# A gated attention and low-rank mixer kernel: the first slot with identity matmuls, smaller first loads and pairs on one engine

## The chip, the cores and the metric

The kernel runs on one core of one Trainium2 chip. The metric is the device time of one execution in microseconds, from its start to its last output; before the change it is 992.4 (median of three runs, 991.75 to 994.2). The engines are TensorE (PE in the profile, with PEld for its weight loads), VectorE (DVE), ScalarE (ACT), GpSimd (POOL) and SyncE (SP), which issues the DMAs. TensorE writes only PSUM; the others work on the on-chip memory, and VectorE and ScalarE read PSUM too.

## The reference, cut to what matters

Batch B = 8, sequence S = 3136, width D = 256, d_qk = 64, rank 32.

```python
def _attn_ref(u, v, z):
    scale = 1.0 / S
    scores = scale * np.matmul(z, z.transpose(0, 2, 1))
    attn = np.maximum(scores, 0.0) ** 2
    out = np.matmul(attn, v)
    return (u * out).astype(np.float32)

def _moe_ref(x, U, V, w_ch1, w_ch2):
    xt = x.transpose(0, 2, 1)
    h = xt @ U @ V
    u = x + h.transpose(0, 2, 1)
    ch = np.maximum(u @ w_ch1, 0.0) @ w_ch2
    return (u + ch).astype(np.float32)
```

The output is `_moe_ref` of `x = _attn_ref(u, v, z)`. The scores of one batch are a symmetric matrix of 3136 x 3136, which is made rectified and squared in bf16 and multiplied with v.

## The kernel before

**Tiles and items.** The sequence is 24 whole tiles of 128 rows and a tail of 64. Four tiles make a group: six groups of 512 columns and one of 64 for each batch. An item is a batch and a group, and the main loop (line 1203) runs through the 56 items; one pass is called a slot. In the slot of item (b, g) TensorE makes AV for that item, that is the squared scores of 512 output rows times v, and, between these matmuls, scores for the items to come and the mixer of items that lie behind. The mixer begins with batch 1, so that the first seven slots have only AV and scores.

**Row halves and ways.** z is kept transposed twice, once in each half of the 128 partitions (`zzT`), so that two matmuls of 64 rows run side by side, on the upper and the lower rows of the array. `pair` (line 173) issues such two. AV also goes in two halves of its 128 inner rows, each crossing two PSUM banks. One assignment of halves to banks is a way. `Ways` (line 567) runs along the 24 tiles in one way, 48 places, and at a turn changes to the other. When the halves change banks, a small GpSimd instruction (`post`, line 164, which shows as `POOLq L168`) stands behind the last matmuls and the next ones wait for it. It stands in GpSimd's own queue, behind any cast issued there before.

**Score pairs.** A score job makes 128 x 1024 scores: two key tiles (the two halves) against the 512 columns of a group. `rectify` (line 350) then writes relu(scale * s) from PSUM as bf16, on ScalarE (line 358) or, when VectorE has the shorter queue by the planner's books, on VectorE (line 354). `square` (line 346) multiplies the result with itself in place, always on VectorE, and is held back until the relu is due. For batch 0, groups 0 to 3, all 12 blocks of a group are made directly (`made_twice`); elsewhere, half of the blocks come from a DMA transpose. For batch 0 the job "last" makes the scores against the tail of the keys.

**The planner.** The program is issued in an order that a planner works out while the kernel is built. `clock` counts TensorE's time in units of one 256-column matmul pair, and `free_at` holds until when each of ScalarE, VectorE and SP is booked. `take_ps` takes the PSUM buffer, of four, that comes free first by these books. `emit` (line 971) goes through the AV places of a slot and issues from three queues what has its place there: `qc` (mixer), `qs` (scores) and `qm` (others). Each entry is a place, how many PSUM buffers must be free, whether the ways turn there, and a function. At a turn (line 979) `emit` also issues some of the `spare` casts on GpSimd: four, or two once the clock is over 200.

**The first slot.** What stands ahead of the main loop (lines 1102 to 1177) loads batch 0: z in three pieces of eight tiles (`first_z`) and v in six pieces of four tiles (`first_v`), all on SP's queue, casts them to bf16 and turns z. A z piece is cast twice (`cast_z`, c = 0 and 1), once for each half of the partitions. z is turned on TensorE: `z_turn` (line 311) multiplies each of eight tiles by the identity `ident` into PSUM and copies 128 x 1024 to `zzT` on ScalarE. Piece 0 is cast by VectorE and ScalarE; v0, z1, v1, v2 and z2 are cast by GpSimd in this order; v3, the tail and v4, v5 are spare casts. Then the first four score pairs come with their engines and times written out by hand (line 1157), then the second `z_turn`, and the planner's clock is set to 90. In slot 0 the other scores stand at places 8, 8, 26, 38, 42, 56, 64, 72, 80 (line 1282) and two each at 16, 46 and nA - 2, where the ways turn; the third and fourth `z_turn` stand at places 22 and 34.

Of the kernel before, what the change touches and what calls it, by code (L numbers as in the profile page):

```python
# [18 lines left out]
def kernel(  # L19
# [11 lines left out]
    nc = tc.nc  # L31
# [85 lines left out]
    def hold(due, f):  # L117
        held.append((due, len(held), f))
# [109 lines left out]
    def z_copy(b, t0, n, raw, c, copy):  # L228
        copy(out=z_bfs[b][:, t0 : t0 + n, c, :], in_=raw[:, : n * dqk].rearrange("p (t d) -> p t d", d=dqk))  # L229
# [18 lines left out]
    def v_copy(b, k, raw, copy):  # L248
        copy(out=v_bfs[b][:, k * GT : (k + 1) * GT, :], in_=raw.rearrange("p (t d) -> p t d", d=D))  # L249
        v_cast.add((b, k))  # L250
# [57 lines left out]
        )  # L308
        queued(NT * P / 4, True)

    def z_turn(b, t0, copy):
        n = min(2 * GT, NT - t0)
        k, pz = take_ps()
        for q in range(n):
            nc.tensor.matmul(  # L315
                out=pz[:, q // GT, (q % GT) * P : (q % GT + 1) * P],
                lhsT=z_bfs[b][:, t0 + q, :, :].rearrange("p c d -> p (c d)"),
                rhs=ident,
                start=(q % GT == 0),
                stop=(q % GT == GT - 1 or q == n - 1),  # L320
            )
        flat = pz.rearrange("p a c -> p (a c)")
        dst = zzTs[b].rearrange("p t c -> p (t c)")[:, t0 * P : (t0 + n) * P]
        copy(out=dst, in_=flat[:, : n * P])  # L324
        pe(8)
        ps_free[k] = book("act", clock[0] + 3, 9.5)
# [19 lines left out]
    def square(a, cost=6.3):  # L346
        book("dve", clock[0], cost)
        nc.vector.tensor_tensor(out=a, in0=a, in1=a, op=ALU.mult)  # L348

    def rectify(dst, src, part=1):  # L350

        ready = clock[0] + 3
        if max(free_at["dve"], ready) + 8 * part < max(free_at["act"], ready):
            nc.vector.tensor_scalar(  # L354
                out=dst, in0=src, scalar1=scale, scalar2=0.0, op0=ALU.mult, op1=ALU.max
            )
            return book("dve", ready, 11.2 if part == 1 else 6.4)
        nc.scalar.activation(out=dst, in_=src, func=AF.Relu, scale=scale)  # L358
        return book("act", ready, 8.7 if part == 1 else 5.3)

    def made_twice(b, g, J):
        return b == 0 and (g <= FIRST or J == g - 1)
# [78 lines left out]
    def score_finish(made):  # L446
        for dst, k, ps, turn, key in made:
            if key and split(*key):
                score_finish_split(dst, k, ps, turn, key)
                continue  # L450
            if turn:
                J, g, b = turn
                unturned[blocks[b, g, J][0]] = False
            done = rectify(dst, ps)
            ps_free[k] = done

            def finish(dst=dst, turn=turn, key=key):
                square(dst)
                if key:
                    squared[key] = squared.get(key, 0) + 1  # L460
                if turn:
                    hold(clock[0] + 7, lambda: ready_turns.append(turn))

            hold(done, finish)

    def score_finish_split(flat, k, ps, h, key):
        if h:
            done = rectify(
                flat[:, 2 * GW : 3 * GW].rearrange("p (j c) -> p j c", c=hw), ps[:, :, :hw], 0.5
            )  # L470
            a, cost = flat[:, 2 * GW : 3 * GW], 3.7
        else:
            done = rectify(
                flat[:, : 2 * GW].rearrange("p (w j c) -> p j w c", w=2, j=2),
                ps.rearrange("p j (w c) -> p j w c", w=2),
            )
# [626 lines left out]
    zraw = [(i * 2 * GT, 2 * GT + (i == 2), *stage_block()) for i in range(3)]  # L1103
    vraw = [stage_block() for _ in range(NQ)]

    def first_v(i):
# [5 lines left out]
    def cast_z(i, c, copy):  # L1112
        t0, n, entry, raw = zraw[i]
        z_copy(0, t0, 2 * GT, raw, c, copy)

    def cast_v(i, copy):
        v_copy(0, i, vraw[i][1], copy)
        give_block(vraw[i][0])

    def cast_tail(copy):  # L1120
        t0, n, entry, raw = zraw[2]
        for c in range(2):
            copy(out=z_bfs[0][:, NF, c, :], in_=raw[:, 2 * GT * dqk : n * dqk])
        v_tail(0, n, raw, copy)
        give_block(entry)

    first_z(0)
# [12 lines left out]
    on_act, on_dve, on_pool = nc.scalar.copy, nc.vector.tensor_copy, nc.gpsimd.tensor_copy  # L1140
    cast_v(0, on_pool)
    cast_z(1, 0, on_pool)
    cast_z(1, 1, on_pool)
    cast_v(1, on_pool)
    cast_v(2, on_pool)
    cast_z(2, 0, on_pool)
    cast_z(2, 1, on_pool)
    spare += [lambda: cast_v(3, on_pool), lambda: cast_tail(on_pool)]
    spare += [lambda i=i: cast_v(i, on_pool) for i in range(4, NQ)]

    cast_z(0, 0, on_dve)
    cast_z(0, 1, on_act)
    clock[0] = 40
    z_turn(0, 0, on_act)
    clock[0] = 58
    made = score_pairs(jobs_of(0, 0)[0:4])
    for (dst, k, ps, _, key), eng, done in zip(made, ("act", "dve", "act", "act"), (73, 79, 82, 92)):
        if eng == "act":
            nc.scalar.activation(out=dst, in_=ps, func=AF.Relu, scale=scale)
        else:  # L1160
            nc.vector.tensor_scalar(out=dst, in0=ps, scalar1=scale, scalar2=0.0, op0=ALU.mult, op1=ALU.max)
        ps_free[k] = done

    def square_first(i):
        dst, _, _, _, key = made[i]
        square(dst)
        squared[key] = squared.get(key, 0) + 1

    square_first(0)
    square_first(1)  # L1170
    z_turn(0, 2 * GT, on_act)
    square_first(2)
    square_first(3)
    for i in range(2):
        give_block(zraw[i][2])
    clock[0] = 90
    free_at.update(act=102, dve=104)

    todo = {t: [] for t in range(n_items)}
    for b in range(B):  # L1180
# [22 lines left out]
    for t in range(n_items):  # L1203
# [68 lines left out]
        elif av:  # L1272
# [105 lines left out]
```

## Time and profile before

| what | value |
|---|---|
| median of three runs | 992.4 us |
| lowest and highest | 991.75 and 994.2 us |
| the profiled execution | 994.29 us |
| its span in the profile | 992.5 us |
| TensorE clock granted | 1.00 in every stage |
| AV of slot 0 multiplied by u (line 694, first row) | starts at 31.40 us |
| the same of slots 1, 2, 3, 4 | 46.09, 59.84, 72.13, 87.02 us |

The span is the time from the first to the last thing that the profile shows; 1.8 us of the execution lie around it. A row of the timeline names the engine, the line of the kernel, the operation, output and input by the program's names, shapes and how many instructions were merged. In brackets stands how long the engine had been idle before the row and what ended that. A busy TensorE is not one at full speed: the rows of TensorE cover a matmul from its start to its modelled end. The granted clock in the profile's stage table is 1.00 from the first microsecond on, so a slow stretch is seen only in the durations of like rows.

### The profile page before, as it was taken

The numbers are of one execution on the slowest core, as the hardware profiler recorded it, in microseconds if no ns is written. First come the engines' busy times: TensorE is split into PE (matmuls) and PEld (weight loads), VectorE is DVE, ScalarE is ACT, GpSimd is POOL, SyncE is SP. The second block draws the span as 40 slices with busy tenths as digits, with TensorE's granted clock in tenths as the row PEclk, the third lists the DMA queues.
The fourth block names the chain that finished last, engine by engine and source line by source line (L and its number), as shares of the span: only waits on it lengthen the run. The fifth ranks groups of instructions, "written<-read, shape, count | busy, mean of one in ns | idle before, by whom it ended". The sixth has DMA issues, their size and how long they took to land.

```text
span 992.5 us, 35366 instructions
## 1 busy us (share of the span) xinstructions
PE 973.9 (98%) x16137; PEld 781.0 (79%) x16137; DVE 618.2 (62%) x793; ACT 491.4 (50%) x584; POOL 17.3 (2%) x24
## 2 busy tenths in 40 slices
PE   6999999999999999999999999999999999999997
PEld 3898788877778777787778877788777877787776
DVE  5977765668556675566756667555765666643453
ACT  5887742457324573355533465434653256422353
POOL 4100000000000000000000000000000000000000
PEclk9999999999999999999999999999999999999999
DMA  7999999889997799787998799975999889964142
GB/s 246 192 213 226 199 205 213 196 145 216 211 181 165 168 215 203 198 139 180 215 213 173 131 192 211 209 169 130 206 230 189 150 170 168 166 123 103 46 110 91
DMA packets 371974, 176.38 MB, mean 178 GB/s; under 512 B 347248, under 2 KB 350320, under 8 KB 371824
## 3 DMA queue, kind: packets, MB, share of 16 engines
q1 hardware_dynamic: 371824, 174.12, 86.8%
q8 instruction: 126, 2.06, 0.9%
q14 instruction: 24, 0.20, 0.1%
HBM read 62.56 MB, written 25.69 MB: 89 GB/s over the span
## 4 chain that ended last, share of the span: by engine, by line
PE 96%; DMA 1%; DVE 1%; ACT 1%; issue 0%; POOL 0%; SPq 0%; POOLq 0%; ACTq 0%
PE ps L178 93%; PE ps L661 1%; PE ps L742 1%; DMA blk<-in_v_dram 1%; DVE blk L348 1%; DMA u2T<-x_bf 0%; ACT blk L358 0%; PE ps L957 0%; ACT blk L906 0%; POOL z_bf L229 0%; DVE blk L354 0%; DVE blk L943 0%; DVE x_bf L694 0%; POOL v_bf L249 0%; PE ps L315 0%
## 5 line engine op out<-in xcount | busy, mean ns | idle before, releaser
L178 PEld LDWEIGHTS <-blk 64*128 64x128 bf16 x12288 | 617.2, 94 | 149.0 <-POOLq L168 7.7
L178 PE MATMUL ps<-v_bf,blk 64*128 64x256 bf16 x9216 | 612.6, 269 | 3.6 <-DVE blk L348 1.8
L358 ACT ACTIVATE blk<-ps 128x1024 bf16<-128x1024 f32 x339 | 319.6, 974 | 365.6 <-PE ps L178 354.2
L348 DVE TENSOR_TENSOR blk<-blk 128x1024 bf16<-128x1024 bf16 x352 | 226.4, 666 | 42.7 <-ACT blk L358 42.1
L178 PE MATMUL ps<-u2T,w_bf 64*128 64x512 bf16 (+1 forms) x1792 | 236.9, 349 | 0.5 <-DMA u2T<-x_bf 0.3
L178 PE MATMUL ps<-w_bf,blk 64*128 64x256 bf16 x3072 | 193.7, 269 | 0.2
L903 DVE TENSOR_SCALAR blk<-ps 128x1024 bf16<-128x1024 f32 (+1 forms) x110 | 127.1, 1155 | 92.9 <-PE ps L178 92.9
L906 ACT ACTIVATE blk<-ps 128x1024 bf16<-128x1024 f32 (+1 forms) x114 | 97.7, 866 | 91.6 <-PE ps L178 91.2
L178 PE MATMUL ps<-zzT 64*128 64x512 bf16 (+2 forms) x902 | 130.2, 329 | 1.7 <-ACT zzT L324 1.7
L178 PEld LDWEIGHTS <-w_bf 64*128 64x128 bf16 x1792 | 90.5, 94 | 29.2 <-POOLq L168 4.1
L694 DVE TENSOR_TENSOR x_bf<-ps,u_sb 128x1024 bf16<-128x1024 f32 x48 | 58.7, 1224 | 70.7 <-PE ps L178 70.7
L815 DVE TENSOR_TENSOR out_sb<-ps,x_bf 128x1024 f32<-128x1024 f32 (+1 forms) x49 | 54.2, 1107 | 59.3 <-PE ps L178 59.3
L943 DVE TENSOR_TENSOR out_sb<-ps,out_sb 128x1024 f32<-128x1024 f32 x42 | 51.3, 1222 | 18.3 <-PE ps L178 18.3
L178 PEld LDWEIGHTS <-zzT 64*128 64x128 bf16 x902 | 41.8, 95 | 8.0 <-ACT zzT L324 2.2
L178 PE MATMUL ps<-t_sb,V_bf 64*128 64x256 bf16 x200 | 20.8, 269 | 0.0
L198 ACT CAST x_bf<-out_sb 128x1024 bf16<-128x1024 f32 (+1 forms) x21 | 17.3, 826 | 6.0 <-DVE out_sb L815 6.0
L200 DVE CAST v_bf<-stage 128x1024 bf16<-128x1024 f32 (+1 forms) x33 | 20.2, 611 | 0.0
L178 PE MATMUL ps<-v_bf,last_sb 64*128 64x256 bf16 x192 | 18.6, 269 | 0.0
L354 DVE TENSOR_SCALAR blk<-ps 128x1024 bf16<-128x1024 f32 (+1 forms) x9 | 10.0, 1106 | 12.9 <-PE ps L178 12.9
L943 DVE TENSOR_TENSOR blk<-ps,blk 128x1024 f32<-128x1024 f32 x6 | 7.3, 1225 | 16.0 <-PE ps L178 15.9
L682 DVE TENSOR_TENSOR u_sb<-ps,u_sb 64x512 f32<-64x512 f32 x8 | 5.5, 682 | 17.1 <-ACT u_sb L680 17.1
L198 ACT CAST v_bf<-stage 128x1024 bf16<-128x1024 f32 x15 | 15.6, 1040 | 0.0
(67 smaller groups left out, 227.7 us busy)
## 6 DMA issues: line engine op xcount, KB each, us to landing
u_sb<-in_u_dram SPq DMA_DIRECT2D x48, 512.0 KB, 5.3
stage<-in_v_dram SPq DMA_DIRECT2D x42, 512.0 KB, 6.2
out_dram<-out_sb SPq DMA_DIRECT2D x42, 512.0 KB, 3.1
stage<-in_z_dram SPq DMA_DIRECT2D x7, 512.0 KB, 6.0
blk<-in_v_dram SPq DMA_DIRECT2D x6, 512.0 KB, 7.1
out_dram<-blk SPq DMA_DIRECT2D x6, 512.0 KB, 2.6
blk<-blk SPq DMA_TRANSPOSE x156, 5.2
blk<-in_moe_w_ch_dram SPq DMA_DIRECT2D x4, 512.0 KB, 5.5
```

The costliest lines, as they stand in the source:

```text
L178: ins = nc.tensor.matmul(**args)
L198: nc.scalar.copy(out=out, in_=in_)
L200: nc.vector.tensor_copy(out=out, in_=in_)
L348: nc.vector.tensor_tensor(out=a, in0=a, in1=a, op=ALU.mult)
L354: nc.vector.tensor_scalar(out=dst, in0=src, scalar1=scale, scalar2=0.0, op0=ALU.mult, op1=ALU.max)
L358: nc.scalar.activation(out=dst, in_=src, func=AF.Relu, scale=scale)
L661: nc.tensor.matmul(out=ps[c * hp : c * hp + rows, h, :D], lhsT=smalls[b][h * hp : (h + 1) * hp, place_of(jt), :], rhs=v_bfs[b][h * hp : (h ...
L694: nc.vector.tensor_tensor(out=xs[b, g][:rows, :n, :], in0=four(box["ps"])[:rows, :n, :], in1=u_sbs[b, g][:rows, :n, :], op=ALU.mult,)
L815: nc.vector.tensor_tensor(out=o[:rows, :n, :], in0=four(ps)[:rows, :n, :], in1=x, op=ALU.add)
L903: nc.vector.tensor_single_scalar(out=r, in_=ps[:, :, :gw], scalar=0.0, op=ALU.max)
L906: nc.scalar.activation(out=r, in_=ps[:, :, :gw], func=AF.Relu)
L943: nc.vector.tensor_tensor(out=o, in0=acc, in1=o, op=ALU.add)
```

## The change

- The z load of the first piece is split into two of four tiles each, the load of the first v piece into two of two tiles each (`load_run`). The two v0 loads go ahead of the second z piece. v4 and v5 go ahead of the first u load.
- Eighteen matmuls of the identity with itself, 128 columns each, are issued on TensorE as soon as the identity is there.
- The first half of z piece 0 is cast by VectorE (c = 0) and ScalarE (c = 1), the second half by VectorE twice. Two `z_turn` of four tiles each take the place of one of eight.
- `rectify` can put a pair whole on one engine, for full pairs of batch 0 that aren't split: VectorE relu and square in one go (`one_pass`), or ScalarE Relu and Square, or as before relu on ScalarE and square on VectorE. It takes the way that ends first by the books.
- The first four pairs go through this choice, and no longer by a list written out by hand. The planner's clock starts at 61 and no longer at 90.
- The second `z_turn` goes from ahead of AV to place 8 of slot 0, with a turn of ways; the third to 32 and the fourth to 58. z piece 2 is cast at place 26 by ScalarE and VectorE, and the tail at place 50 by VectorE, and no longer by GpSimd.
- In slot 0 the ways turn at places 8, 24, 40, 56, 72 and 88, with one score pair at each from 24 on; ten more pairs stand between. One spare cast is issued at each turn in slot 0, and two in later slots.
- `cast_v` for batch 0 casts a piece in two halves.

```diff
-    def z_turn(b, t0, copy):
-        n = min(2 * GT, NT - t0)
+    def z_turn(b, t0, copy, n=2 * GT):
+        n = min(n, NT - t0)
...
-    def rectify(dst, src, part=1):
+    def rectify(dst, src, b, part=1, whole=False):
 
         ready = clock[0] + 3
-        if max(free_at["dve"], ready) + 8 * part < max(free_at["act"], ready):
+        dve, act = max(free_at["dve"], ready), max(free_at["act"], ready)
+        if whole and not b:
+            slow = 10 if slot[0] == 0 else 6.3
+            ends = {"dve": dve + DVE, "act": act + 17.4, "both": max(act + 8.7, dve) + slow}
+            way = min(ends, key=lambda w: ends[w])
+            if way == "dve":
+                return one_pass(dst, src, ready)
+            if way == "act":
+                nc.scalar.activation(out=dst, in_=src, func=AF.Relu, scale=scale)
+                nc.scalar.activation(out=dst, in_=dst, func=AF.Square)
+                done = book("act", ready, 8.7)
+                book("act", ready, 8.7)
+                return done, free_at["act"]
+        elif dve + 8 * part < act:
...
+    DVE = 20
+
+    def one_pass(dst, src, ready):
+
+        nc.vector.tensor_scalar(out=dst, in0=src, scalar1=scale, scalar2=0.0, op0=ALU.mult, op1=ALU.max)
+        done = book("dve", ready, 11.2)
+        square(dst, 9)
+        return done, free_at["dve"]
...
-                for f in spare[: 2 if clock[0] > 200 else 4]:
+                for f in spare[: 2 if slot[0] else 1]:
...
+    for h in range(2):
+        load_run(zraw[0][3], z[0], dqk, h * GT, GT)
     make_identity(nc, ident)
+    for h in range(2):
+        load_run(vraw[0][1], v[0], D, h * GT // 2, GT // 2)
     first_z(1)
-    first_v(0)
     first_v(1)
     first_v(2)
     first_z(2)
     first_v(3)
     load_tail(zraw[2][3], 2 * GT * dqk, z[0], dqk)
     load_tail(zraw[2][3], (2 * GT + 1) * dqk, v[0], D)
+    first_v(4)
+    first_v(5)
     load_u(*items[0])
-    for i in range(4, NQ):
-        first_v(i)
...
+    spare += [lambda i=i: cast_v(i, on_pool) for i in range(1, NQ)]
+
+    k, ps = take_ps()
+    for _ in range(18):
+        nc.tensor.matmul(out=ps[:, 0, :P], lhsT=ident, rhs=ident, start=True, stop=True)
+    ps_free[k] = 36
+    cast_z(0, 0, on_dve, 0, GT)
+    cast_z(0, 1, on_act, 0, GT)
+    for c in range(2):
+        cast_z(0, c, on_dve, GT, 2 * GT)
...
+    clock[0] = 38
+    z_turn(0, 0, on_act, GT)
+    z_turn(0, GT, on_act, GT)
+    clock[0] = 46
+    free_at.update(dve=46, act=51)
+    jobs0 = jobs_of(0, 0)
+    score_burst(jobs0[:1])
+    score_burst(jobs0[1:2])
+    clock[0] = 52
+    score_burst(jobs0[2:3])
+    clock[0] = 54
+    score_burst(jobs0[3:4])
+    clock[0] = 61
...
             if t == 0:
-                at = [8, 8, 26, 38, 42, 56, 64, 72, 80]
-                for i, x in ((2, 22), (3, 34)):
-                    qm.append((x, 0, False, lambda i=i: z_turn(0, i * 2 * GT, on_act)))
+                at, k = [16, 18, 28, 44, 50, 64, 68, 78, 84, 92], 0
+                qs += [(x, 0, True, lambda: scores(1)) for x in (24, 40, 56, 72, 88)]
+                qm.append((8, 0, True, lambda: z_turn(0, 2 * GT, on_act)))
+                qm.append((26, 0, False, lambda: (cast_z(2, 0, on_act), cast_z(2, 1, on_dve), book("act", 0, 5.7), book("dve", 0, 4))))
+                qm.append((32, 0, False, lambda: z_turn(0, 4 * GT, on_act)))
+                qm.append((50, 0, False, cast_tail))
+                qm.append((58, 0, False, lambda: z_turn(0, 6 * GT, on_act)))
             qs += [(x, 1, False, lambda: scores(1)) for x in at]
-            qs += [(x, k, True, lambda: scores(k)) for x in (16, 48 if t else 46, nA - 2) if k]
+            qs += [(x, k, True, lambda: scores(k)) for x in (16, 48, nA - 2) if k]
```

More of the change, by code (lines that the diff above doesn't have):

```diff
@@ L453, in score_finish, with finish @@
                 unturned[blocks[b, g, J][0]] = False
-            done = rectify(dst, ps)
+            done, whole = rectify(dst, ps, key[0] if key else 0, whole=True)
             ps_free[k] = done
-            def finish(dst=dst, turn=turn, key=key):
-                square(dst)
+            def finish(dst=dst, turn=turn, key=key, whole=whole):
+                if whole is None:
+                    square(dst)
                 if key:
@@ L461, in finish @@
                 if turn:
-                    hold(clock[0] + 7, lambda: ready_turns.append(turn))
-            hold(done, finish)
+                    hold(clock[0] + (7 if whole is None else 1), lambda: ready_turns.append(turn))
+            hold(whole or done, finish)
     def score_finish_split(flat, k, ps, h, key):
         if h:
-            done = rectify(
-                flat[:, 2 * GW : 3 * GW].rearrange("p (j c) -> p j c", c=hw), ps[:, :, :hw], 0.5
+            done, _ = rectify(
+                flat[:, 2 * GW : 3 * GW].rearrange("p (j c) -> p j c", c=hw), ps[:, :, :hw], key[0], 0.5
             )
@@ L1104 @@
     vraw = [stage_block() for _ in range(NQ)]
+    on_act, on_dve, on_pool = nc.scalar.copy, nc.vector.tensor_copy, nc.gpsimd.tensor_copy
     def first_v(i):
@@ L1110, in first_z, with cast_z, cast_tail, load_run @@
         load_z_piece(0, *zraw[i][:2], zraw[i][3], tail=False)
-    def cast_z(i, c, copy):
+    def cast_z(i, c, copy, lo=0, hi=2 * GT):
         t0, n, entry, raw = zraw[i]
-        z_copy(0, t0, 2 * GT, raw, c, copy)
+        z_copy(0, t0 + lo, hi - lo, raw[:, lo * dqk :], c, copy)
     def cast_v(i, copy):
-        v_copy(0, i, vraw[i][1], copy)
+        raw = vraw[i][1].rearrange("p (t d) -> p t d", d=D)
+        for h in range(0, GT, GT // 2):
+            copy(out=v_bfs[0][:, i * GT + h : i * GT + h + GT // 2, :], in_=raw[:, h : h + GT // 2, :])
+        v_cast.add((0, i))
         give_block(vraw[i][0])
-    def cast_tail(copy):
+    def cast_tail():
         t0, n, entry, raw = zraw[2]
         for c in range(2):
-            copy(out=z_bfs[0][:, NF, c, :], in_=raw[:, 2 * GT * dqk : n * dqk])
-        v_tail(0, n, raw, copy)
+            on_dve(out=z_bfs[0][:, NF, c, :], in_=raw[:, 2 * GT * dqk : n * dqk])
+        v_tail(0, n, raw, on_dve)
+        book("dve", clock[0], 5)
         give_block(entry)
-    first_z(0)
+    def load_run(raw, a, w, t0, n):
+        nc.sync.dma_start(
+            out=raw[:, t0 * w : (t0 + n) * w].rearrange("p (t d) -> p t d", d=w), in_=rows_of(a)[:, t0 : t0 + n, :]
+        )
+    for h in range(2):
+        load_run(zraw[0][3], z[0], dqk, h * GT, GT)
     make_identity(nc, ident)
+    for h in range(2):
+        load_run(vraw[0][1], v[0], D, h * GT // 2, GT // 2)
     first_z(1)
-    first_v(0)
     first_v(1)
```

37 lines of the change are left out of this document (4 added, 33 removed).

## The prediction, made before the change was run

> **What bounds the kernel now.** I read the page first, then busy time by stage, then the timeline of the first 35 us engine by engine, then the list of what TensorE waited for. The page's first line says who sets the time:
>
> ```profile
> PE 973.9 (98%) x16137; PEld 781.0 (79%) x16137; DVE 618.2 (62%) x793; ACT 491.4 (50%) x584; POOL 17.3 (2%) x24
> ```
>
> TensorE idles 992.5 − 973.9 = 18.6 us. The stages (columns: time, then busy us and instructions of PE, PEld, DVE, ACT, POOL; clock, DMA share, GB/s) say where:
>
> ```profile
> 0.00:12.30 12.30, 3.90 (x26) 1.98 (x28) 5.45 (x6) 5.77 (x6) 4.81 (x10) 1.00 0.83 274
> 12.30:31.00 18.70, 17.28 (x242) 12.24 (x243) 13.80 (x17) 14.35 (x15) 7.59 (x10) 1.00 0.75 192
> 31.00:46.00 15.00, 14.07 (x229) 11.91 (x227) 13.77 (x19) 13.59 (x15) 4.85 (x5) 1.00 1.03 216
> 46.00:72.00 26.00, 25.96 (x438) 23.61 (x434) 20.58 (x31) 23.42 (x24) 0.00 (x0) 1.00 0.99 218
> 106.00:112.10 6.10, 4.33 (x72) 3.32 (x69) 4.18 (x7) 5.71 (x6) 0.00 (x0) 1.00 0.84 215
> ```
>
> Idle are 8.4 us before 12.3, 1.4 in the rest of slot 0, 0.9 in slot 1, nothing from 46 to 106, 1.8 just before 112.1. Those 12.5 us, and matmuls that run slowly although busy, are all that a rewrite of the first slot can touch. TensorE's early rows (start, us, form, count, what ended the idle time):
>
> ```profile
> 4.06 1.03 PE L315 MATMUL ps<-ident,z_bf 128*128 128x128 bf16 x8 [4.06 <-ACT z_bf L229]
> 6.20 1.89 PE L178 MATMUL ps<-zzT 64*128 64x512 bf16 x8 [1.10 <-ACT zzT L324]
> 11.32 1.03 PE L315 MATMUL ps<-ident,z_bf 128*128 128x128 bf16 x8 [3.23 <-POOL z_bf L229]
> 12.29 1.89 PE L178 MATMUL ps<-v_bf,blk 64*128 64x256 bf16 x16
> 17.33 0.62 PE L315 MATMUL ps<-ident,z_bf 128*128 128x128 bf16 x8
> 19.28 1.04 PE L178 MATMUL ps<-v_bf,blk 64*128 64x256 bf16 x16
> 33.87 0.28 PE L178 MATMUL ps<-v_bf,blk 64*128 64x256 bf16 x2 [0.93 <-DVE blk L348]
> ```
>
> The same 16 AV matmuls take 1.89 us at 12.3 and 1.04 at 19.3, the same eight transposes 1.03 and 0.62: TensorE is slow until about 15.4, some 4.1 us after its work became continuous at 11.3. AV could start at 9.65, when the first square ends, but stands in the program behind a z transpose that waits for GpSimd:
>
> ```profile
> 8.19 1.04 POOL L249 CAST v_bf<-blk 128x1024 bf16<-128x1024 f32 x1 [6.89 <-DMA blk<-in_v_dram]
> 9.17 2.09 POOL L229 CAST z_bf<-blk 128x512 bf16<-128x512 f32 x2
> 8.42 4.83 DVE L348 TENSOR_TENSOR blk<-blk 128x1024 bf16<-128x1024 bf16 x4
> 30.20 1.28 DVE L348 TENSOR_TENSOR blk<-blk 128x1024 bf16<-128x1024 bf16 x2
> ```
>
> The last two rows are squares: 1.21 us each while GpSimd casts, 0.64 when it doesn't.
>
> **The change, part by part, in us from the span's start.**
>
> *First loads.* The first z load is issued at 0.74 and its cast starts at 3.39. Half of it cannot land before the issue of bytes began moving (about 1.75) nor later than the whole: 2.3 to 3.4; I take 3.05, because the second 1-us slice already moved 277 GB/s. Casts of 128x256 are not in the trace; 128x512 takes 0.43 (DVE) and 0.62 (ACT), so between half and all of that: 0.25 and 0.40. First half cast: 3.5. Four transposes instead of eight, slow: between half and all of 1.03, 0.6, so 4.15; ACT copy of half the width, between 0.5 and 1.01: 0.6, so 4.8. Score pair 0 starts at 4.85, not 6.20. Pair to relu took 0.65 (6.20 to 6.85): relu at 5.5. The second half (0.6 transposes, 0.6 copy) ends at 5.4, behind which pairs 2 and 3 run at about 5.7 and 6.1. SP issues two more DMAs (0.42 each), so the z and v pieces behind leave up to 0.85 later; bytes, not issues, limit them (0.3 MB a us from 2 on), so nothing, at most 0.85.
>
> *Pair on one engine.* By the hand-set clocks, pairs 0 and 2 go whole to ScalarE, 1 and 3 whole to VectorE, then about alternately. ScalarE's Square is not in the trace. Nearest rows: its relu of the same size, 0.95 each where three take 2.85 in a row, and its cast from the same memory, 1.05: I take 0.95, range 0.9 to 1.05. ScalarE: relu 5.5, square to 7.4, relu 2 and square to 9.25. VectorE: 1.23 + 0.64 (1.21 against GpSimd): pair 1 done at 7.8, pair 3 at 9.65. **AV starts at 7.45** instead of 12.29. Of "ScalarE: Activation LUTs" in the Trainium skill, the rules for kernel authors speak against this: products belong on VectorE. By the uncontended 0.64 that holds, each ScalarE square loses 0.3, 3 us over the ten in this slot; by the contended 1.21 it gains 0.26. Both engines have idle time here, so the sum takes neither.
>
> *GpSimd.* The casts of v0 go in halves, then z1 (2.1 contended, 1.17 free). v0 lands at 8.14 now as the third load behind 0.5 MB; its halves now have 0.25 MB ahead, so they land between 4.2 and 8.1; I take 5 and 6.3, z1 at about 7, cast by 8.6. v1 to v5 now go one at each turn of ways, behind the semaphore instruction of that turn; AV behind a turn waits for that instruction, and it waits for the cast of the turn before: 1.04 to 1.47 against 1.7 and more between turns, so nothing, unless a v piece lands late, whose rest of the wait TensorE would then see whole. The u load goes behind v4 and v5 on SP, some 1 to 2 us later; it is read at 28: nothing.
>
> *Identity matmuls.* The identity is ready at 1.30; eighteen at 1.03/8 = 0.13 at most fill 1.35 to 3.3 to 3.7, beside the z load, so they delay nothing by more than 0.2. With transposes and scores TensorE is then nearly continuous from 1.35 to 6.7, longer than 4.1: I take AV at full speed from 7.45. If not, the first 16 AV matmuls and eight transposes cost 0.85 + 0.41 more.
>
> *Order in slot 0* (place = number of AV pairs out, 0.107 each; a score pair 0.215). Places 0 to 7 end at 8.4 to 8.75; z transpose to 9.3; its copy on ScalarE (free at 9.25) to 10.3; scores at 16 and 18 at 10.4; place 28 at 12.4; place 32 at 13.0. There stands the next transpose, and its input's cast is queued on ScalarE behind relu and square of two pairs: 10.85 + 4 × 0.95 + 0.6 = 15.25. **TensorE waits 2.25.** This is where most of the earlier start goes. Copy to 16.9; places 32 to 39 beside it. From 16.95: 56 places × 0.107 = 6.0; 11 score pairs, 2.4; four turns of ways at about 0.2 (the rows show 0.17 to 0.28 for the GpSimd semaphore); tail transpose 0.2; the "last" scores wait 1.25, since the tail's copy is behind a pair on ScalarE until 22.3; 0.55 for a PSUM buffer near place 88; AV's end 0.2. That makes 28.2 to 28.3 against 30.87 now: **−2.5**. Bounds: −4.8 if the 2.25 are not met, 0 if the chain slips as in the second rival. The casts that leave GpSimd (z2, tail) cost 0.62 on ScalarE and about 1 on VectorE, counted above.
>
> *Slot 1.* The 0.93 at 33.87 is a wait for squares behind a VectorE backlog (23.5 to 33.8 almost without a gap). VectorE now holds fewer squares; place 16's blocks are done by about 31.2, before they are read. I take **−0.7**, bounds −0.93 and +0.5.
>
> *Slots 2 to 6.* The new choice between engines holds there too; TensorE waits for nothing from 46 to 106 now, covered by 2.6 us of idle ScalarE and 5.4 of VectorE between 46 and 72. Nothing, loss up to 1.
>
> *112.1.* The 1.77 are a v cast on ScalarE behind three relus and a w cast. Which engine takes it depends on bookings that shift. **−0.3**, bounds −1.77 and +1.
>
> Sum −3.5: span 989.0, this execution (994.3 for a span of 992.5) 990.8, and from the median of 992.4, which I use below, **988.9**.
>
> **Rivals.**
>
> 1. *ScalarE is earlier at place 32*, because whole pairs leave no engine waiting for the other. For it: ScalarE idles 2.7 us before 12.39 and 1.2 before 14.64 now. Against: four serial ScalarE instructions stand before the cast. The 2.25 go, perhaps part of the 1.25 too: 988.9 − 2.25 to −3 = 986.3.
> 2. *v0 and z1 land no earlier.* The DMA engines are 0.9 busy from 2 us on and v0 took 6.5 from issue to landing. Then the z transpose stands at 11.3 as now, the chain slips 2.6, and only slots 1 and 112 give: 992.4 − 1.0 + 0.6 for three turns more = 992.0.
> 3. *Slower: TensorE goes cold again.* After 3.24 us idle the 11.32 row ran slowly. If the wait at place 32 is 4.0 and not 2.25 (deciding at about 3.2), it adds 1.75, and 4.1 us of half speed add 2.05; the waits in slot 1 and at 112 stay (1.0): 992.4 + 1.3 = 993.7; met again at "last", another 2 to 4.
> 4. *Square needs another table.* The trace has one table load, 1.28 us, and no Square. Ten whole pairs with two loads each cost ScalarE 25.6 in slot 0; less some 7 of idle, the end is about 15 later, near 1007. "ScalarE: Activation LUTs" (section on table sets) says functions come in sets, cheap ones in every set, and a switch costs about 2.7 us; by that Square, if cheap, reloads nothing. No run here shows it yet.
>
> That the identity matmuls warm nothing is inside the first case: +1.3.
>
> **Chances.** Forecast 0.47 (its own range 986.5 to 991), rival 1 0.23, 2 0.15, 3 0.10, 4 0.05. 0.3%, 3.0 us, is about what a measurement of this kernel tells from no change; below 989.4 lie two thirds of the forecast and rival 1: 0.55. Above 995.4 lie rival 4 and most of rival 3: 0.12. The rest is 0.33. The range 985.5 to 994 leaves out rival 4, half of rival 3 and the far end of rival 1: under 0.2.
>
> **What would show it.** First score pair at 4.85, AV at 7.45 with sixteen matmuls in about 1.04 there; Square near 0.95 and one table load; a TensorE wait of about 2 us for a z cast on ScalarE near 13; slot 0's AV product multiplied out near 28.7 instead of 31.4; no wait near 31 to 34. Wrong is the forecast if AV starts after 9, if TensorE waits over 3 us after its start, or if slots 2 to 6 show new waits.

## The result, and the profile after

The change makes the kernel slower: 998.67 us (median of six runs, 997.73 to 999.19) against 992.83 (six runs, 991.75 to 994.2), a ratio of 1.0054 with a 95% interval of 1.0044 to 1.0065, so 4.4 to 6.5 us. The forecast was 988.9. The profiled execution of the changed kernel took 997.73 with a span of 996.0; that of the kernel before took 994.29 and 992.5. The six runs spread over 1.5 us here and 2.5 before. The profiled execution is the shortest of the six here and, before, longer than any of the six, so the two profiles differ by 3.5 us where the medians differ by 5.8.

The page's first line and two of its stages (columns as before):

```profile
PE 975.2 (98%) x16155; PEld 784.3 (79%) x16155; DVE 619.7 (62%) x793; ACT 498.4 (50%) x592; POOL 14.2 (1%) x25
...
31.00:46.00 15.00, 11.81 (x176) 8.94 (x171) 11.00 (x14) 12.72 (x15) 3.90 (x5) 1.00 0.67 161
46.00:72.00 26.00, 24.59 (x410) 22.20 (x409) 21.65 (x29) 24.88 (x26) 0.00 (x0) 1.00 0.97 235
```

TensorE idles 3.2 us between 31 and 46, where it idled 0.9, and 1.4 between 46 and 72, where it idled nothing. ScalarE has 7 us more work in all. The timeline of TensorE, cut to the rows that answer to those of before:

```profile
7.36 1.05 PE L178 MATMUL ps<-v_bf,blk 64*128 64x256 bf16 x16 [0.70 <-ACT blk L362]
9.76 0.62 PE L315 MATMUL ps<-ident,z_bf 128*128 128x128 bf16 x8 [1.35 <-POOL z_bf L229]
16.59 0.62 PE L315 MATMUL ps<-ident,z_bf 128*128 128x128 bf16 x8 [2.25 <-ACT z_bf L229]
33.09 0.61 PE L178 MATMUL ps<-v_bf,blk 64*128 64x256 bf16 x8 [0.27 <-ACT blk L362]
35.11 0.72 PE L178 MATMUL ps<-v_bf,blk 64*128 64x256 bf16 x10 [1.41 <-DVE blk L348]
45.78 0.39 PE L178 MATMUL ps<-zzT 64*128 64x512 bf16 x2 [1.04 <-ACT blk L371]
46.69 0.39 PE L178 MATMUL ps<-zzT 64*128 64x512 bf16 x2 [0.52 <-ACT blk L371]
59.96 0.39 PE L178 MATMUL ps<-zzT 64*128 64x512 bf16 x2 [0.89 <-ACT blk L371]
```

AV starts at 7.36 and no longer at 12.29, and at full speed. At place 8 TensorE waits 1.35 us for GpSimd's cast of z1, which runs from 8.04 to 9.71. The wait of 2.25 for the cast of z2 on ScalarE is there. New are the waits of slot 1, for squares (33.09, 35.11) and for PSUM buffers that a relu has not yet emptied (45.78, 46.69), and one of the same kind in slot 2 (59.96). The product with u that ends slots 0 and 1:

```profile
30.29 1.22 DVE L713 TENSOR_TENSOR x_bf<-ps,u_sb 128x1024 bf16<-128x1024 f32 x1
49.20 1.23 DVE L713 TENSOR_TENSOR x_bf<-ps,u_sb 128x1024 bf16<-128x1024 f32 x1 [0.83 <-PE ps L178]
```

Slot 0 ends 1.1 us earlier (31.40 before). Slot 1 takes 18.9 us where it took 14.7, and hands over 3.1 us late. TensorE idles 3.7 us of it, where it idled 0.9. Slots 2 to 6 together add 0.85 (from 49.20 to 119.92 against 46.09 to 115.96).

The chain of waits through slot 0 (start, us, what) tells whose work sets it:

```profile
11.92 1.03 ACT blk L361
...
12.97 1.06 ACT blk L362
14.03 0.92 ACT blk L361
...
14.97 1.06 ACT blk L362
16.03 0.52 ACT z_bf L229
...
16.59 0.63 PE ps L315 x8
17.25 1.02 ACT zzT L324
...
19.40 1.03 ACT blk L361
...
20.46 1.06 ACT blk L362
21.51 0.92 ACT blk L361
...
22.46 1.06 ACT blk L362
```

L361 and L362 are the relu and the square of a whole pair. From 11.9 to 23.5 the chain hardly leaves ScalarE; TensorE appears in it twice, for 0.63 and 1.06 us, each time between two of ScalarE's tasks. Ahead of it stand the load of z1 and GpSimd's cast of it, up to 9.71. In slot 1 the chain goes through VectorE's whole pairs (relus at 32.50 and 41.55, squares behind them) and two relus on ScalarE at 44.72. ScalarE's groups from 4 to 49 us (form, count, busy us, mean ns) and VectorE's largest group of relus, first of the changed kernel, then of the one before:

```profile
L362 ACT ACTIVATE blk<-blk 128x1024 bf16<-128x1024 bf16 x13 | 13.7, 1057 | 0.4
L361 ACT ACTIVATE blk<-ps 128x1024 bf16<-128x1024 f32 x13 | 13.2, 1018 | 5.1 <-PE ps L178 2.9 <-issue 2.2
L371 ACT ACTIVATE blk<-ps 128x1024 bf16<-128x1024 f32 x9 | 8.6, 1018 | 0.0
L378 DVE TENSOR_SCALAR blk<-ps 128x1024 bf16<-128x1024 f32 x12 | 14.7, 1222 | 9.8 <-PE ps L178 9.7
```

```profile
L358 ACT ACTIVATE blk<-ps 128x1024 bf16<-128x1024 f32 x29 | 28.1, 1047 | 5.8 <-PE ps L178 4.6 <-issue 0.8
L1159 ACT ACTIVATE blk<-ps 128x1024 bf16<-128x1024 f32 x3 | 2.9, 1024 | 0.7 <-PE ps L178 0.7
L354 DVE TENSOR_SCALAR blk<-ps 128x1024 bf16<-128x1024 f32 x3 | 3.7, 1225 | 4.8 <-PE ps L178 4.8
```

Thirteen squares stand on ScalarE, 13.7 us, and it makes 22 relus of whole pairs of tiles where it made 32. VectorE makes twelve relus of blocks (1.22 each) where it made four, the three shown and one of the list written out by hand. From 4 us to the end of slot 1, ScalarE and VectorE were busy 31.9 + 32.7 = 64.6 us before, and are now busy 37.8 + 32.5 = 70.3.

### The profile page after: what moved, and what is told of

The parts are those of the page before. It is cut to its first block, busy times and chain, and to the rows that moved or that the text cites. A ratio compares the mean times of both kernels' runs of the same rounds, so it can differ in the third digit from the quotient of the medians.

```text
span 996.0 us, 35415 instructions
## 1 busy us (share of the span) xinstructions
PE 975.2 (98%) x16155; PEld 784.3 (79%) x16155; DVE 619.7 (62%) x793; ACT 498.4 (50%) x592; POOL 14.2 (1%) x25
## 4 chain that ended last, share of the span: by engine, by line
PE 94%; ACT 3%; DMA 1%; DVE 1%; issue 1%; SPq 0%; POOL 0%; POOLq 0%; ACTq 0%; DVEq 0%
PE ps L178 92%; PE ps L680 1%; PE ps L761 1%; ACT blk L371 1%; ACT blk L361 1%; DMA blk<-in_z_dram 1%; ACT blk L362 1%; PE ps L976 0%; ACT blk L925 0%; DVE blk L348 0%; DVE blk L378 0%; ACT zzT L324 0%; DMA blk<-in_moe_V_dram 0%; SPq L1153 0%; POOL z_bf L229 0%
## 5 line engine op out<-in xcount | busy, mean ns | idle before, releaser
L371 ACT ACTIVATE blk<-ps 128x1024 bf16<-128x1024 f32 (+1 forms) x316 | 296.9, 965 | 358.1 <-PE ps L178 354.6
L348 DVE TENSOR_TENSOR blk<-blk 128x1024 bf16<-128x1024 bf16 x336 | 212.7, 652 | 46.3 <-ACT blk L371 45.1
L922 DVE TENSOR_SCALAR blk<-ps 128x1024 bf16<-128x1024 f32 (+1 forms) x110 | 127.1, 1155 | 92.2 <-PE ps L178 92.2
L925 ACT ACTIVATE blk<-ps 128x1024 bf16<-128x1024 f32 (+1 forms) x114 | 97.7, 866 | 91.6 <-PE ps L178 88.8
L178 PEld LDWEIGHTS <-zzT 64*128 64x128 bf16 x902 | 42.3, 94 | 13.7 <-issue 5.9
L378 DVE TENSOR_SCALAR blk<-ps 128x1024 bf16<-128x1024 f32 x17 | 20.8, 1222 | 10.6 <-PE ps L178 10.5
L361 ACT ACTIVATE blk<-ps 128x1024 bf16<-128x1024 f32 x16 | 16.3, 1020 | 5.6 <-PE ps L178 3.4
L178 PE MATMUL ps<-v_bf,last_sb 64*128 64x256 bf16 x192 | 18.6, 269 | 0.1
L362 ACT ACTIVATE blk<-blk 128x1024 bf16<-128x1024 bf16 x16 | 16.9, 1057 | 0.5
```

Of the source, the lines that this page charges most:

```text
L178: ins = nc.tensor.matmul(**args)
L362: nc.scalar.activation(out=dst, in_=dst, func=AF.Square)
L378: nc.vector.tensor_scalar(out=dst, in0=src, scalar1=scale, scalar2=0.0, op0=ALU.mult, op1=ALU.max)
L922: nc.vector.tensor_single_scalar(out=r, in_=ps[:, :, :gw], scalar=0.0, op=ALU.max)
L925: nc.scalar.activation(out=r, in_=ps[:, :, :gw], func=AF.Relu)
```

## The experiments

All were run in five rounds beside the kernel before on the same chip. The first four share a median of before of 993.88 us, the next four 993.71, the next four 993.12 and the last two 994.0. The batches ran on three chips, so runs of different batches are compared by their ratios. The end of a slot is the start of its product with u, in the profile. There is one profile of each, and one thing in it differs from execution to execution: the transposes of z1 at place 8 start at 9.76 in the first profile of the changed kernel and at 8.39 in that of e14, the same program. A slot end of one profile can be off by a microsecond for that alone.

| run | median us | ratio to before, 95% | slot 0 ends | slot 1 ends |
|---|---|---|---|---|
| the changed kernel | 998.67 | 1.0054 (1.0044 to 1.0065) | 30.29 | 49.20 |
| e1 whole pairs in slot 0 alone | 996.28 | 1.0024 (1.0015 to 1.0034) | 32.30 | 50.27 |
| e2 no whole pairs | 992.15 | 0.9983 (0.9975 to 0.9992) | 28.96 | 45.22 |
| e3 before, whole pairs from slot 1 | 996.17 | 1.0026 (1.0017 to 1.0035) | 31.61 | 47.51 |
| e4 z2 and tail cast on GpSimd | 994.54 | 1.0010 (1.0001 to 1.0019) | 27.38 | 44.66 |
| e5 first four pairs whole | 990.16 | 0.9967 (0.9957 to 0.9976) | 27.60 | 42.54 |
| e6 e5 and e4 together | 988.78 | 0.9953 (0.9940 to 0.9967) | 26.66 | 41.20 |
| e7 one identity matmul | 998.54 | 1.0054 (1.0040 to 1.0068) | 30.98 | 49.88 |
| e8 fewer turns of ways | 999.65 | 1.0061 (1.0047 to 1.0076) | 32.08 | 50.45 |
| e9 half squares on ScalarE | 993.95 | 1.0012 (1.0002 to 1.0022) | 28.24 | 45.80 |
| e10 prices as measured | 995.20 | 1.0020 (1.0010 to 1.0030) | 29.39 | 45.51 |
| e11 no later ScalarE squares | 992.00 | 0.9996 (0.9986 to 1.0006) | 28.03 | 43.89 |
| e12 e6, one identity matmul | 989.00 | 0.9960 (0.9946 to 0.9974) | 28.77 | 43.30 |
| e13 kept warm | 997.80 | 1.0049 (1.0035 to 1.0062) | 30.14 | 49.04 |
| e14 the changed kernel again | 998.50 | 1.0051 (1.0038 to 1.0063) | 30.29 | 49.19 |

**e1.** The new choice in slot 0 alone.

```diff
-        if whole and not b:
+        if whole and not b and slot[0] == 0:
```

> The changed kernel with the choice of putting a pair whole on one engine left to slot 0 alone; from slot 1 on the old choice. Theory A (whole pairs cost more engine time than split ones, 2.0 us on ScalarE or 1.9 on VectorE against 0.97 + 0.64, and slots 1 and 2 run out of ScalarE and VectorE): slot 1's AV product starts near 47 instead of 49.2, slot 2's near 62, and the time falls by 2 to 4 us against the changed kernel, to about 995. Rival B (slot 0 itself hands slot 1 a backlog, through its own whole pairs and the casts taken off GpSimd): slot 1 still takes 18 us or more and the time stays within 1 us of the changed kernel, 998.

The time falls by about 3 us (1.0024 against 1.0054), as theory A said, but slot 1 still takes 18.0 us, as rival B said. Both hold in part: slot 0's whole pairs hand a backlog on, and the later ones add to it. Slot 1 does not end near 47, as theory A had it; part of that is a slow stretch of TensorE in this profile, shown under e13 and e14.

**e2.** No whole pair anywhere.

```diff
-        if whole and not b:
+        if False and whole:
```

> The changed kernel with no pair whole on one engine anywhere: relu on one engine and square on VectorE, as before. Theory A (engine time): the ten squares on ScalarE and as many relus on VectorE of slot 0 go too, slot 0 ends by 29 and slot 1's AV product starts by 45; the time is at or below the kernel before, 989 to 993. Rival B (order of slot 0, and the wait of 2.25 us for the z cast on ScalarE): slot 0 ends no earlier than 30 and the time stays above 995.

992.15, 0.17% under before: everything else in the change together is a small gain. AV starts at 8.89, because the first squares come later, and slot 0 still ends at 28.96. Rival B alone is out.

**e3.** The kernel before with the changed `rectify` and `score_finish`, the choice open from slot 1 on.

```diff
+        if whole and not b and slot[0]:
```

> The kernel before, with the new choice for batch 0 from slot 1 on and nothing else of the change. Theory A: slot 1 gets longer by 1 to 3 us, slots 2 to 5 by another 0 to 2, and the time rises to 994 to 997. Rival B (the choice is harmless outside slot 0): within 1 us of the kernel before, 992 to 994.

+2.3 us (996.17 against 993.88) on a kernel whose first slot is the old one: the later whole pairs cost that by themselves.

**e4.** The casts of z piece 2 and of the tail go back to GpSimd.

```diff
...
-    spare += [lambda i=i: cast_v(i, on_pool) for i in range(1, NQ)]
+    spare += [lambda: (cast_v(1, on_pool), cast_z(2, 0, on_pool), cast_z(2, 1, on_pool))]
+    spare += [lambda: (cast_v(2, on_pool), cast_tail())]
+    spare += [lambda i=i: cast_v(i, on_pool) for i in range(3, NQ)]
...
-                qm.append((26, 0, False, lambda: (cast_z(2, 0, on_act), cast_z(2, 1, on_dve), book("act", 0, 5.7), book("dve", 0, 4))))
...
-                qm.append((50, 0, False, cast_tail))
```

> The changed kernel with the casts of z piece 2 and of the tail back on GpSimd, behind v1 and v2. Rival B (the casts on ScalarE and VectorE and the wait at place 32 do the harm): the wait of 2.25 us before the third transpose goes, slot 0 ends near 28 and the time falls by 2 us or more, to 996 or less. Theory A: the wait goes too, but slot 1 takes back at least half of it, and the time falls by 0.5 to 1.5 us, to about 997.

The wait of 2.25 is gone, slot 0 ends at 27.38 and the time falls by some 4.4 us, twice what rival B asked for. That the casts and the wait behind them do harm is shown; theory A's number was too small. In this profile z1 came earlier too (transposes at 8.95 against 9.76), so not all of the 2.9 us of slot 0 are the casts'. Slot 1 still takes 17.3 us, so they aren't all of the loss.

**e5.** Whole pairs for the first four score pairs only; a flag is lowered behind them.

```diff
-        if whole and not b:
+        if whole and not b and first[0]:
...
     score_burst(jobs0[3:4])
+    first[0] = False
```

> The changed kernel with only the first four pairs whole on one engine; every later pair in the old way. Theory A (a whole pair costs 2.0 us on ScalarE or 1.9 on VectorE against 1.6 shared, and the engines run out in slots 0 to 2; the first four cost nothing, as both engines wait there): AV starts at 7.4 as in the changed kernel instead of 8.89 without any whole pair, slot 1's AV product starts at 44 to 45, and the time is 991 to 992, no more than in the kernel without whole pairs (992.15) and 6 us or more under the changed kernel. Rival B (the whole pairs of the prelude hand the backlog on): slower than without whole pairs by 1 us or more.

990.16, some 1.6 us under the kernel without any whole pair (0.9967 against 0.9983), 3.3 under before and 8.5 under the changed kernel (0.9967 against 1.0054). So the thirty later whole pairs, 14 on ScalarE and 16 on VectorE, cost 8.5 us. Where both engines wait for work anyway, a whole pair is a gain. The busy time from 4 us to the end of slot 1 in the kernel before, the changed one and e5, one row of each (columns as in the stages above):

```profile
4.00:46.10 42.10, 35.35 (x491) 26.24 (x493) 32.68 (x40) 31.91 (x35) 16.55 (x18) 1.00 0.92 228
```

```profile
4.00:49.20 45.20, 34.37 (x487) 24.17 (x489) 32.50 (x40) 37.82 (x41) 13.51 (x19) 1.00 0.87 224
```

```profile
4.00:42.50 38.50, 35.57 (x493) 24.26 (x495) 31.94 (x42) 32.99 (x37) 15.36 (x19) 1.00 0.95 246
```

e5 does the same slots with 64.9 us of ScalarE and VectorE in 38.5 us, the changed kernel with 70.3 in 45.2. TensorE's busy time is alike. By the end of slot 1 the early start is worth 3.6 us when no work is added (42.50 against 46.10); the change adds 5.7 us of work and gives back more than that.

**e6.** e5 and e4 together.

> The same, and the casts of z piece 2 and of the tail on GpSimd behind v1 and v2. If the wait at place 32 is TensorE's own loss (rival B), it adds its 2.25 us again: 989 to 990. If ScalarE and VectorE set the pace (theory A), it gives what leaves them, 2 us of casts on two engines, so about 1: 990 to 991.

988.78 (0.9953): the fastest, 4.9 us under before on the same chip and 10 under the changed kernel. The casts give another 1.4, between the two numbers. In this profile the first AV matmuls run slowly (1.89) and still slot 0 ends at 26.66.

**e7.** One identity matmul for eighteen, in the changed kernel.

> The changed kernel with one identity matmul instead of eighteen. Theory C (they bring TensorE to full speed for the start of AV): the first sixteen AV matmuls take 1.9 us instead of 1.05, TensorE stays slow to 11 or later, and the time rises by 0.5 to 1.5 us, to 999.5. Theory A with the engines as the bound from place 16 on: slow TensorE is hidden behind ScalarE, and the time stays within 0.5 us of the changed kernel.

No change in the median (1.0054 both), although in the profile the first sixteen AV matmuls take 1.89 and not 1.05 and the transposes behind them 1.04 and not 0.62. Theory C's 0.5 to 1.5 us are not seen. That the slow matmuls are hidden behind ScalarE is not shown: both slots end 0.7 us later in this profile (30.98 and 49.88), which is within the spread of the runs.

**e8.** In the changed kernel the scores at places 40 and 72 come without a turn.

> The changed kernel with the ways turned at places 8, 24, 56 and 88 of slot 0 instead of also at 40 and 72. Theory A: two semaphore waits of about 0.2 us less on TensorE, hidden behind the engines: within 0.5 us of the changed kernel. Rival D (turning every 16 places lets AV use blocks twice before it needs new ones, so fewer turns starve it): slot 0 waits for squares or v casts that it doesn't wait for now, 1 to 3 us more.

The interval overlaps that of the changed kernel. In the profile slot 0 waits 0.41 and 0.76 us more for squares, which is rival D's mechanism, but the medians differ by a microsecond and an effect is not shown. The 1.8 us by which slot 0 ends later here are not the turns' alone: TensorE's clock is at half from 16.2 to 19.6 in this profile. The turns are not what made the change slow, since fewer of them don't make it faster.

**e9.** ScalarE's Square on half of each pair; one key tile of the two stays unsquared.

```diff
-                nc.scalar.activation(out=dst, in_=dst, func=AF.Square)
+                nc.scalar.activation(out=dst[:, 0], in_=dst[:, 0], func=AF.Square)
```

> The changed kernel, same program and same order of everything, but ScalarE's Square covers only the first of a pair's two key tiles (512 of 1024 columns; the other half stays unsquared, so part of the computation is left out). It takes about 0.43 us from each of the sixteen ScalarE squares and nothing else. Theory A (ScalarE's and VectorE's time is what the time goes to): slot 0 ends near 28, slot 1's AV product starts at 47 or earlier, and the time falls by 2 us or more, to 996.5 or less. Rival E (the order does it: the planner's books, overdrawn at the end of slot 0, place AV and scores badly in slot 1): the waits of slot 1 stay, and the time falls by less than 1 us.

The same program in the same order, each square 0.63 and not 1.06 us: 16 x 0.43 = 6.9 us less of ScalarE. The time falls by 4.2 to 4.7 us (1.0012 against 1.0054), and slot 1 ends at 45.80:

```profile
16.21 1.01 ACT L324 CAST zzT<-ps 128x1024 bf16<-128x1024 f32 x1 [0.71 <-PE ps L315]
18.37 1.02 ACT L361 ACTIVATE blk<-ps 128x1024 bf16<-128x1024 f32 x1 [1.14 <-PE ps L178]
19.42 0.63 ACT L362 ACTIVATE blk<-blk 128x512 bf16<-128x512 bf16 x1
```

The copy of the third z transpose starts at 16.21 where it starts at 17.25 in the changed kernel: the squares queued ahead of it are shorter. Two such squares make 0.86 of that microsecond. This is the cleanest reading of theory A, since the other runs that change the choice also change the planner's books and with them the order; that order (rival E) is at most what is left.

**e10.** The choice by prices as measured.

```diff
-            ends = {"dve": dve + DVE, "act": act + 17.4, "both": max(act + 8.7, dve) + slow}
+            ends = {"dve": dve + DVE, "act": act + 18.9, "both": max(act + 8.7, dve) + slow}
...
-    DVE = 20
+    DVE = 17.5
```

with `slow = 6.3` throughout and the same numbers in the books.

> The changed kernel, whole pairs still allowed everywhere in batch 0, but chosen by prices as measured: ScalarE whole 18.9 units (2.02 us) and not 17.4, VectorE whole 17.5 (1.87 us) and not 20, square on VectorE 6.3 and not 10 in slot 0. If the choice is only mispriced (rival F), the time falls to that with the first four alone, 990 to 991. Theory A (any pair put whole costs engine time, whatever it ends at, since the choice looks at this pair's end and not at what is left for the next): some of it stays, 993 to 996.

995.2, within theory A's range: 3.4 us of the loss go with right prices, 5 stay against e5. This fits a choice that looks at this pair's end alone and doesn't see what it takes from the next, but no run isolates that.

**e11.** After the first four pairs a pair goes whole to VectorE or is shared, never whole to ScalarE.

```diff
+            if not first[0]:
+                ends.pop("act")
             way = min(ends, key=lambda w: ends[w])
```

> The changed kernel with ScalarE's squares only in the first four pairs; after that a pair goes whole to VectorE or is shared. Theory A puts most of the loss on ScalarE's squares (0.4 us of engine time each, and a ScalarE that is held for 2 us when a cast or a copy is due) and some on the rest: 993 to 996. If ScalarE's squares are all of it: 990 to 991. If VectorE's whole pairs are as bad: 997 or more.

992.0: ScalarE's later squares make some 5 to 6 us of the loss, VectorE's later whole pairs some 3 (0.9996 against 0.9967 of e5). Below the range that theory A gave, so ScalarE's part is larger than expected, but not all. The two parts are rough: VectorE has nine later whole pairs here and sixteen in the changed kernel.

**e12.** e6 with one identity matmul.

> The kernel with only the first four pairs whole and the z2 and tail casts on GpSimd (988.8 in the run before), with one identity matmul instead of eighteen. Theory C: with ScalarE and VectorE no longer the bound of slot 0, slow matmuls at the start of AV show in the time: 0.5 to 1.5 us more, 989.3 to 990.3. Theory A alone (still hidden): within 0.4 us, 988.4 to 989.2.

989.0 against 988.8, in two batches, with overlapping intervals: what the identity matmuls are worth can't be told from nothing even here. The profile is that of the longest of the six runs (990.86); it has a wait of 1.7 us for the first z cast in place of them, and slot 0 ends at 28.77.

**e13 and e14.** The changed kernel with 20 and 36 more identity matmuls where it waits at places 8 and 32, and the changed kernel itself.

```diff
+    warm = {(0, 2 * GT): 20, (0, 4 * GT): 36}
...
+        for _ in range(warm.get((b, t0), 0)):
+            nc.tensor.matmul(out=pz[:, 0, :P], lhsT=ident, rhs=ident, start=True, stop=True)
         for q in range(n):
```

> The changed kernel with 20 more identity matmuls ahead of the z transpose at place 8 and 36 ahead of the one at place 32, where TensorE waits anyway (1.35 and 2.25 us in the changed kernel's profile). Rival 3 of the prediction (TensorE's clock falls again in slot 0 and that is part of the loss): no stage of the profile is granted 0.50, and the time falls by 1 us or more against the changed kernel on the same chip. Theory A alone (slow matmuls are hidden behind ScalarE): within 0.5 us of it.

> The changed kernel itself, beside the run with more identity matmuls on the same chip. Rival 3: its runs spread by a microsecond or more with the clock granted, and a profile may show 0.50 for some microseconds in slot 0. Theory A alone: no spread that goes with the clock; about 998.7.

The medians are 997.8 and 998.5, with intervals that overlap. In e14's profile the clock is granted at half for some 3 us, in slot 0 (the last three columns are the clock, the DMA share and GB/s):

```profile
15.00:16.00 1.00, 0.58 (x6) 0.59 (x7) 0.70 (x2) 0.36 (x1) 0.00 (x0) 0.59 1.00 397
16.00:17.00 1.00, 1.00 (x13) 0.62 (x11) 0.00 (x0) 0.52 (x1) 0.00 (x0) 0.50 1.01 396
```

Yet slots 0 and 1 end at 30.29 and 49.19, as in the profile whose clock did not fall there (30.29, 49.20). That is two differences that cancel. Three rows of e14's timeline of TensorE:

```profile
8.39 0.62 PE L315 MATMUL ps<-ident,z_bf 128*128 128x128 bf16 x8
15.41 1.03 PE L315 MATMUL ps<-ident,z_bf 128*128 128x128 bf16 x8 [2.25 <-ACT z_bf L229]
16.38 1.89 PE L178 MATMUL ps<-v_bf,blk 64*128 64x256 bf16 x16
```

In e14 GpSimd casts z1 from 6.34 on and not from 8.04, TensorE does not wait at place 8, and the third transposes start 1.18 us earlier than in the first profile (15.41 against 16.59). Then they and the AV matmuls behind them run slowly (1.03 and 1.89 against 0.62 and 1.05), and at 18.98 both profiles are level. So the third rival did happen, at the end of a wait of 2.25 us, and cost slot 0 some 1.2 us of this execution. In e1's profile the clock is at half for longer, from about 9.2 to 16.1, and slot 0, the same program as in the changed kernel, ends 2 us later. One profile of each is little. By the medians of e13 and e14 the part that more identity matmuls win back is 0.7 us and can't be told from nothing, and against a loss of 5.8 it is not the cause. Both runs spread over more than 2 us. What makes that spread stays open: e13's two long runs have the lower mean clock (0.999 against 1.0), e14's have not.

## Why the prediction was wrong, point by point

**First loads, first pairs, AV's start: right, but for z1.** AV starts at 7.36 (forecast 7.45) at full speed, v0 landed as estimated, and rival 2 is out. The full speed is partly luck: with the same eighteen identity matmuls the first sixteen AV matmuls took 1.89 us in the profiles of e5, e6, e9 and e11. The cast of z1 was forecast to end by 8.6 and ended at 9.71, so that TensorE waited 1.35 us at place 8 for what the sum put at nothing.

**Square on ScalarE: at the upper end of its range, its weight wrong.** 1.06 us in this profile against 0.95 taken and 1.05 as the upper end, and 2.0 for a whole pair. There is one table load in all, for sixteen Squares between relus, so rival 4 is out. The Trainium skill's rule that cheap functions are in every set ("ScalarE: Activation LUTs", table sets) fits, if Square is one of them: the rule's own list does not name it.

**The step that failed** is the sentence at the end of "Pair on one engine": both engines have idle time in this slot, "so the sum takes neither" the loss of 0.3 us for each square nor the gain, and the same for the slots behind. Idle time of an average was taken for time that is free where it is needed. The runs show 8.5 us in its place: e5, which makes no pair whole past the first four, is faster than the changed kernel by that. By the slot ends of the two profiles, slot 0 is 2.7 us shorter in e5, slot 1 4.0 and slots 2 to 6 together 1.1. ScalarE and TensorE wait for each other in turn, and a longer square delays the z cast, the copy of the transposes, the next relu and the PSUM buffer behind it. e9 shows it with the order unchanged: 6.9 us less of squares, 4.2 to 4.7 us less of time. The rule of the Trainium skill that products belong on VectorE ("ScalarE: Activation LUTs", rules for kernel authors) was cited there as one that speaks against the change. By the uncontended row it gave 3 us over ten squares; that is the right sign for this term, though it would only have brought the forecast to −0.5. Nine squares ran on ScalarE in slot 0, but 16 in all, and the seven later ones were not counted.

**Order in slot 0: right in kind, short in size.** The wait at place 32 is 2.25 us, as worked out, at 16.59 and not 15.25, and the wait for the tail's copy 1.30 (forecast 1.25). The slot's product starts at 30.29 and not 28.7: it is 1.1 us earlier than before and not 2.7. Of the 1.6 us that are missing, 1.34 are there at the third transposes already, and 1.0 of these comes from z1 (its transposes start at 9.76 where 8.75 was forecast). In e14, where z1 came early, the third transposes start at 15.41, close to the forecast of 15.25, and the fall of the clock takes the lead back. Rival 1, in which ScalarE is free earlier and the wait goes, did not happen; e4, which takes the cast off ScalarE, removes the wait and gains 4.4 us, more than its length.

**Slot 1: wrong by 4.9 us, the largest miss.** −0.7 was taken, with +0.5 as the worst end; it is +4.2. The argument was that VectorE holds fewer squares at the slot's start. What it holds instead are relus at 1.22 each, ScalarE holds squares, and both reach slot 1 with pairs in hand that AV needs at once.

**Slots 2 to 6: +0.85 in the profile,** in the range (up to 1) but not the value; the new wait of 0.89 at 59.96 is one of the signs of a wrong forecast that the prediction named. e3 has a total of 2.3 us for all later whole pairs on the old first slot.

**Rival 3, TensorE goes cold again: not the cause, but real.** The prediction took 3.2 us of idle time as what decides. In e14 the clock fell during the wait of 2.25 us.

**112.1: 1.8 us of waiting for the same v cast stand in every run.** The −0.3 did not come.

**Sum in runs:** −3.5 was forecast, +5.8 measured. Without whole pairs past the first four (e5) the change is worth −3.3 by its ratio, within 0.2 us of the forecast. That closeness is partly luck: in e5's profile slot 0 ends 3.8 us earlier (forecast 2.7), slot 1 takes 0.25 longer (forecast 0.7 shorter), and the wait at 112 stays. The term set to nothing decided the sign.

## What to carry to other kernels

Two engines that are busy for 50% and 62% of a kernel can still be the bound of a stage: add up the work of both, from the first use to the end of that stage, before and after, and count work that is moved to a dearer engine as added. Ending this piece of work soonest is a poor rule for a choice of engine where the queue behind it is long; it pays only where the engines wait, as in the first four pairs. If a stage's chain lies on another engine, removing one instruction from that engine can gain more than the wait it explains. Warming TensorE brought nothing that the medians show here (e7, e12, e13), though a slow stretch cost slot 0 some 1.2 us in e14's profile.

## What was not expected of the hardware

TensorE's granted clock fell back to half in several profiles of kernels with the identity matmuls, after waits of no more than 2.25 us and at different times in the same program: not in slot 0 of the changed kernel's first profile, from 15.2 to 18.6 us in the second. In the rows of the first microseconds the matmuls ran at half speed while the stage table gave 1.00, and in e5's profile the AV matmuls at 7.41 still did (1.89 us), so there the table can't be taken at its word. VectorE's square took 0.62 to 0.69 us in most rows and up to 1.21 beside GpSimd's casts; yet at 8.54 and 13.61 in the changed kernel it took 0.69 beside a cast too, so what decides stays open. ScalarE's took 1.06 in all sixteen rows.
